# First difference of relu'd blocks kept in its PSUM bank, the transposes of the next batch moved into second products, weight stores at other times

## The chip, the cores and the metric

The kernel runs on one core of one Trainium2 chip. The metric is device time in microseconds (us) of one launch. The kernel before took 1024.24, 1024.7 and 1025.53 us in three runs; their median is 1024.7.

The engines have the names of the profile: PE multiplies matrices (PEld loads its weights), DVE and ACT work elementwise and can read and write PSUM, POOL works elementwise on SBUF, SP issues the transfers (DMA). PSUM has eight banks that matmuls of 128 x 384 results use here.

## The reference

Four batches of 768 tokens, eight heads of 64. Attention is restricted to keys of the query's own cluster; its result, heads side by side, is the input x (768 x 512 for each batch) of a second layer:

```
q_assign, k_assign = nearest of 16 centroids, by cosine
scores = where(q_assign == k_assign, q @ k.T / 8, -1e9)
x = softmax(scores) @ v                       # (4, 768, 512)
u = x + ((x.T @ U) @ V).T                     # mixes tokens, rank 32
out = u + maximum(u @ w1, 0) @ w2             # w1: 512 x 2048, w2: 2048 x 512
```

All is fp32. The kernel gets that precision out of the faster fp32r matmul by splitting an operand into a high and a low half, and adds three products (high x high, high x low, low x high).

## The kernel before, in words

The engines work in the order in which the program issues instructions to them; nothing reorders them. `at(time, fn, args)` puts a call into a plan, the plan is sorted by time, and the calls run in that order. The unit of the plan's time is one hidden chunk of the dense feed-forward (about 4.2 us, as 32 of them with their surroundings make up 466 to 635.7 us of the span); `M0` is that stage's start, `o` the start of a batch behind it. A plan's time decides order alone: an instruction starts when its engine reaches it and what it waits for is done.

There are three stages. **Attention**, 0 to 466 us, isn't touched. **Dense feed-forward of batch 0**, 466 to 635.7 us: in two halves of 384 tokens, 16 hidden chunks each, `gemm1` (L592), `after_gemm1` (L603: ReLU and split) and `gemm2` (L610) follow one another. Beside it the weights of the groups g = 2 and 3 are rebuilt from 64-bit words (`load_weights`, L178: joins on DVE at L162 to L172, high half on ACT at L190, low half on DVE at L191). Beside it, too, weights are prepared for the third stage. **Batches 1 to 3**, 635.7 to 1018 us, are computed by seven products on 2 x 2 blocks (Strassen in Winograd's form) instead of eight.

*Weights for the seven products.* For each of eight pairs n = 0 to 7 (group g, matrix k), `recover` (L656) adds high and low halves of four blocks (ACT copies one to PSUM at L659, DVE adds the other at L660), `combine` (L662) forms four sums on POOL, `split_high` (L673, ACT) and `split_low` (L678, POOL, L680) split them, `store_sum` (L682) stores them to DRAM from SP. Plain blocks are stored by `store_block` (L641). The sums lie in a buffer `f` in two places: even n and n = 7 share one, so that n = 7 waits for n = 6's stores. `fetch_w1` and `fetch_w2` bring the stored weights back, for one K at a time.

*Tokens for the seven products.* `fetch_half` brings 384 tokens of the next batch into the one buffer `st`; `turn_half` (L739) transposes them, three transposes a call into a bank (L742) and a copy by ACT (L743). `u_sums` (L749, DVE), and `u_halves` (L757: high half on ACT, low half on POOL, L761 and L766) form four sums and all halves of the seven left blocks. The first products need them in the order B11, T2, T3, T1, B21, T4, B22.

*A batch.* K counts eight blocks of hidden units. First products (1,K): seven groups of six matmuls (`seven1`, L799 to L801), one bank each. `after1` (L803) adds products with one another on DVE as they come; the results are the four relu'd blocks of hidden values, B11 and B22 through an ACT ReLU into SBUF, B12 and B21 left raw in their banks. `h_sums` (L834) then forms T1 = relu(B12) - B11, T3 = relu(B12) - B22, T2 = B22 - T1, T4 = relu(B21) - T2 on DVE (L838), and `h_halves` (L840) splits the seven blocks (ACT the high half, L845 and L848; the low half DVE for B21, L846, POOL for the others, L849). Second products (2,K): seven groups of six matmuls (`seven2`, L863 to L865), whose results `after2` (L872) adds to the output on DVE (L883) or copies at the first K of some accumulators on ACT (L881). The order in a batch is (1,0) (1,1) (1,2) (2,0) (1,3) (2,1) (1,4) (2,2) (1,5) (2,3) (1,6) (2,4) (1,7) (2,5) (2,6) (2,7). After the batch eight joins (`join_up`, L910, on DVE and POOL) make its output blocks; they stand in the first part of the next batch.

*Banks.* `bank()` (L730) hands the eight PSUM banks out in rotation, to product groups and, in batches 1 and 2, to the transposes of the next batch. A group waits until the bank's former tenant has been read for the last time: so the eighth call after raw B22's needs B22's bank, and each `turn_half` among them makes that an earlier group. `ring()` (L726) does the same for SBUF buffers of 128 x 384, and `spare` hands out pairs of buffers for high and low halves.

Of the kernel before, what the change touches and what calls it, by code (L numbers as in the profile page):

```python
# [34 lines left out]
AF = mybir.ActivationFunctionType  # L35
# [82 lines left out]
def clustered_attention_moe(ctx: ExitStack, tc: tile.TileContext, qk, v, cen, moe_U, moe_V, w1, w2, out):  # L118
# [3 lines left out]
    nc = tc.nc  # L122
# [570 lines left out]
    def pieces(x, n):  # L693
        return [x[:, k * n:(k + 1) * n] for k in range(x.shape[1] // n)]
# [21 lines left out]
    def open_right():  # L716

        pool["w3"].close()
        right = ctx.enter_context(tc.tile_pool(name="right", bufs=1, side="right", reuse_waits="tile"))
        acc = [rows.tile([P, 2, 2, HS], F32, name="acc", tag="R"), right.tile([P, 2, 2, HS], F32, name="acc2")]  # L720
        pool["acc"] = {key: acc[k // 2][:, k % 2] for k, key in enumerate((B11, T1, T3, T2))}
        pool["ring"] += pieces(right.tile([P, 4 * HS], F32, name="ring"), HS)
        spare.extend(pool["h"])
        spare.extend(right.tile([P, 2, HS], F32R, name=f"h{k}") for k in range(7))

    def ring():  # L726
        count["f"] += 1
        return pool["ring"][count["f"] % len(pool["ring"])]
# [74 lines left out]
    def after1(b, K, s):  # L803

        key = order[0][s]
        ps = live.pop(("p", b, K, key))
        h = live.setdefault(("f", b, K), {})
        add = nc.vector.tensor_add
        if key == B11:
            h["s"] = ring()  # L810
            nc.scalar.copy(h["s"], ps)
        elif key == T2:
            h["a"] = ring()
            add(h["a"], ps, h["s"])
        elif key == T3:
            h["b"] = ring()
            add(h["b"], ps, h["a"])
        elif key == T1:
            add(h["a"], ps, h["a"])
            add(ps, ps, h["b"])  # L820
            h["2"], h[B22] = ps, ring()
            nc.scalar.activation(h[B22], ps, AF.Relu)
        elif key == B21:
            add(ps, ps, h["s"])
            h[B11] = h["s"]
            nc.scalar.activation(h[B11], ps, AF.Relu)
        elif key == T4:
            add(ps, ps, h["b"])
            h[B21] = ps
        else:  # L830
            add(ps, ps, h["a"])
            h[B12] = ps

    def h_sums(b, K, key):  # L834
        h = live["f", b, K]
        one, two = {T1: (B12, B11), T3: (B12, B22), T2: ("2", T1), T4: (B21, T2)}[key]
        h[key] = ring()
        nc.vector.scalar_tensor_tensor(out=h[key], in0=h[one], scalar=0.0, in1=h[two], op0=ALU.max, op1=ALU.subtract)  # L838

    def h_halves(b, K, key):  # L840
        x = live["f", b, K][key]
        out_ = live["h", b, K, key] = spare.pop(0)
        hi, lo = out_[:, 0], out_[:, 1]
        if key == B21:
            nc.scalar.activation(hi, x, AF.Relu)  # L845
            nc.vector.scalar_tensor_tensor(out=lo, in0=x, scalar=0.0, in1=hi, op0=ALU.max, op1=ALU.subtract)  # L846
        else:
            nc.scalar.copy(hi, x)  # L848
            nc.gpsimd.tensor_sub(lo, x, hi)  # L849

    def unit2(b, e):
# [167 lines left out]
        at(m + (16.35 if i == 0 else 16.47), finish, i)  # L1019

    for n_, (g, k) in enumerate((g, k) for g in range(NG) for k in range(2)):
        c = M0 + 1.5 + 3.2 * n_
        for r in range(4):
            at(c + 0.4 * r, recover, n_, k, g, r)
            at(c + (0.9, 1.4, 1.75, 2.1)[r], combine, n_, r)
            at(c + (1.9, 2.25, 2.6, 2.8)[r], split_high, n_, r)
            at(c + (2.4, 2.7, 3.0, 3.3)[r], split_low, n_, r)
            at(c + (2.8, 3.1, 3.4, 3.7)[r], store_sum, n_, k, g, r)
        for r, name in enumerate(("A11", "A12", "A22")):
            for half in range(2):  # L1030
                x = 2 * r + half
                since = (95, 142, M0 - 9, M0 - 2.5)
                at(since[n_] + (6 if g == 0 else 0.9) * x if g < 2 else M0 + 1 + 4.1 * (n_ - 2) + 0.65 * x,
                   store_block, k, g, name, half)

    at(M0 + 18, open_sevens)
# [3 lines left out]
    for b in range(1, B):  # L1040
        o = M0 + NF * nh + 28 * (b - 1)
        if b == 1:
            fetched, turns = (o - 13.9, o - 6.4), (o - 7.7, o - 5.4)
        else:
            fetched, turns = (o - 20, o - 14), (o - 17.2, o - 9.7)
        for h in range(2):
            at(fetched[h], fetch_half, b, h)
            for d in range(ND):
# [9 lines left out]
        for k, (which, x) in enumerate(seq):  # L1058
# [7 lines left out]
                    at(t + U * s, seven2, b, m, e)  # L1066
                    at(t + U * s + 0.27, after2, b, m, e)
            if which == 1:
                for key, when_ in ((B22, 1.2), (B11, 1.45), (B21, 1.7)):
                    at(t + when_, h_halves, b, x, key)  # L1070
                for r, key in enumerate((T1, T3, T2, T4)):
                    at(t + 1.81 + 0.14 * r, h_sums, b, x, key)
                    at(t + (2.0, 2.15, 2.3, 2.56)[r], h_halves, b, x, key)
                if x + 2 < 8 or b < B - 1:
                    for s0, s1 in ((0, 4), (4, 7)):
                        at(t + U * s1 + 0.02, fetch_w1, (x + 2) % 8, s0, s1)
# [7 lines left out]
                at(o + 28 + when_, join_up, b, j)  # L1084
    for K in range(2):
        for s0, s1 in ((0, 4), (4, 7)):
            at(M0 + 23 + K, fetch_w1, K, s0, s1)
            at(M0 + (29.5 + 0.5 * K if s0 == 0 else 31.8 + 0.1 * K), fetch_w2, K, *range(s0, s1))

    plan.sort(key=lambda event: event[:2])  # L1090
    for _, _, fn, args in plan:
# [31 lines left out]
```

## Time and profile before

| | |
|---|---|
| median of three runs | 1024.7 us |
| profiled execution, its own time | 1025.75 us |
| its span | 1024.0 us |
| granted clock of PE, mean | 0.977 |
| busy PE / DVE / POOL / ACT | 962.9 / 709.2 / 624.1 / 471.5 us |
| DMA | 205.28 MB, 200 GB/s mean |

Rows of groups read: line of the kernel, engine, operation, what it writes <- what it reads, size, count, then busy time and the mean of one, then the engine's idle time just ahead of such instructions and what ended most of it. In a timeline a row begins with its start and its length, and ends in brackets with the idle time ahead of it and its releaser. Tiles have the program's names: ps_p and ps_q are the two name groups of the eight banks, st, f, u, h, hx, w, ring, rw, rw_g, rw_t SBUF buffers (several are buffers of earlier work used again), wc the stored weights in DRAM, u_scr the tokens in DRAM. Granted clock is the share of full speed that PE had in that stretch. Sums over stages hide much: PE's idle time is in few places, so it is read stretch by stretch.

### The profile page before, as it was taken

What the parts mean: (1) busy time and instruction counts of PE and PEld (TensorE: products, weight loads), DVE (VectorE), ACT (ScalarE), POOL (GpSimd) and SP (SyncE); (2) the same over time, 40 slices, a digit from 0 to 9 for tenths busy, and PEclk for the clock granted to TensorE, in tenths of its full rate; (3) what the DMA queues carried; (4) which work ended last, traced back from release to release, by engine and by line L of the source; (5) the groups of instructions that cost most, each with busy time, mean ns of one, the idle gap of its engine ahead of it and who ended that gap; (6) DMA issues with size and microseconds to landing.
All of it is one profiled execution on the core that took longest, in us unless ns stands there. A gap on an engine that the chain in (4) does not pass through costs nothing. (4 is left out here: it accounts for less than half of the span.)

```text
span 1024.0 us, 15360 instructions
## 1 busy us (share of the span) xinstructions
PE 962.9 (94%) x5368; PEld 785.0 (77%) x5368; DVE 709.2 (69%) x1298; ACT 471.5 (46%) x837; POOL 624.1 (61%) x477
## 2 busy tenths in 40 slices
PE   5899999999999999988898999999899998999997
PEld 3666676666667666656676879999899998999997
DVE  5797777777777767677867424746497665876767
ACT  4454554555556554564555434543244432344330
POOL 5466676988788967753545757634286533767431
PEclk9899999999999999989999999999999999999999
DMA  7754654656475646254688995775568775777743
GB/s 183 193 129 109 161 145 106 198 157 160 123 223 150 151 114 196 73 192 127 216 294 271 298 329 216 246 278 206 216 220 294 273 272 178 254 261 259 261 145 143
DMA packets 76732, 205.28 MB, mean 200 GB/s; under 512 B 8624, under 2 KB 42416, under 8 KB 71792
## 3 DMA queue, kind: packets, MB, share of 16 engines
q1 hardware_dynamic: 73968, 195.82, 59.9%
q10 hardware_dynamic: 2688, 8.49, 2.8%
q8 instruction: 42, 0.69, 0.3%
q14 instruction: 34, 0.28, 0.1%
HBM read 131.07 MB, written 41.94 MB: 169 GB/s over the span
## 5 line engine op out<-in xcount | busy, mean ns | idle before, releaser
L479 POOL TENSOR_TENSOR T<-T,pr 128x768 f32<-128x768 f32 x120 | 226.5, 1887 | 46.7 <-ACT pr L469 20.5
L442 DVE TENSOR_REDUCE m<-ps_max 128x1 f32<-128x384 f32 x384 | 195.3, 548 | 84.0 <-PE ps_max L440 82.4
L469 ACT ACTIVATE pr<-st 128x768 f32<-128x768 f32 x192 | 154.4, 812 | 86.2 <-PE st L466 69.5
L440 PE MATMUL ps_max<-arena 128*128 128x384 f32 x384 | 127.2, 381 | 6.7 <-DVE oh L356 2.5
L487 PE MATMUL o_ps<-pr,vt 128*64 128x384 f32 x768 | 133.1, 497 | 0.1
L464 PE MATMUL st<-arena 128*128 128x384 f32 x384 | 105.9, 357 | 1.8 <-ACT pr L469 1.8
L440 PEld LDWEIGHTS ps_max<-arena 128*128 128x128 f32 x384 | 70.9, 193 | 45.2 <-issue 22.0
L487 PEld LDWEIGHTS o_ps<-pr,vt 128*64 128x64 f32 x768 | 53.0, 139 | 67.1 <-issue 61.3
L466 PE MATMUL st<-arena 97*128 97x384 f32 x384 | 100.2, 343 | 3.7 <-DMA arena<-mT 1.9
L479 POOL TENSOR_TENSOR T<-pr 128x768 f32<-128x768 f32 x30 | 56.5, 1885 | 64.2 <-ACT pr L469 64.2
L464 PEld LDWEIGHTS st<-arena 128*128 128x128 f32 x384 | 66.8, 192 | 17.7 <-issue 9.9
L466 PEld LDWEIGHTS st<-arena 97*128 97x128 f32 x384 | 70.8, 191 | 5.7 <-issue 3.9
L491 ACT COPY os<-o_ps 128x384 f32<-128x384 f32 x32 | 15.3, 479 | 105.6 <-PE o_ps L487 105.6
L799 PE MATMUL ps_p<-arena,w 128*128 128x384 f32 x178 | 59.8, 336 | 0.0
L801 PE MATMUL ps_p<-arena,w 128*128 128x384 f32 x178 | 59.6, 335 | 0.0
L800 PE MATMUL ps_p<-arena,w 128*128 128x384 f32 x178 | 59.6, 335 | 0.0
L799 PE MATMUL ps_q<-arena,w 128*128 128x384 f32 x158 | 53.6, 339 | 0.0
L801 PE MATMUL ps_q<-arena,w 128*128 128x384 f32 x158 | 52.9, 335 | 0.0
L800 PE MATMUL ps_q<-arena,w 128*128 128x384 f32 x158 | 52.9, 335 | 0.0
L849 POOL TENSOR_TENSOR h<-ring,h 128x384 fp32r<-128x384 f32 x21 | 21.5, 1031 | 36.0 <-ACT h L848 19.5
L380 POOL TENSOR_TENSOR arena<-R,arena 128x768 fp32r<-128x768 f32 x18 | 34.5, 1923 | 13.6 <-ACT arena L375 8.0
L607 DVE SCALAR_TENSOR_TENSOR hx<-ps_h,hx 128x384 fp32r<-128x384 f32 x32 | 17.7, 553 | 27.4 <-ACT hx L606 27.2
(479 smaller groups left out, 2462.3 us busy)
## 6 DMA issues: line engine op xcount, KB each, us to landing
w<-wc SPq DMA_DIRECT2D x24, 1024.0 KB
w<-wc SPq DMA_DIRECT2D x24, 768.0 KB
wc<-f SPq DMA_DIRECT2D x52, 256.0 KB
arena<-wc SPq DMA_DIRECT2D x17, 768.0 KB
R<-in_qk SPq DMA_DIRECT2D x32, 384.0 KB
arena<-arena SPq DMA_DIRECT2D x32, 384.0 KB
arena<-arena SPq DMA_DIRECT2D x64, 192.0 KB
arena<-wc SPq DMA_DIRECT2D x10, 1024.0 KB
```

Source lines behind the costliest of these rows:

```text
L380: eng.tensor_sub(part(X2[i % 3], 0, h), live["R", i][:, 2 * h:2 * h + 2].rearrange("p j q -> p (j q)"), part(X1[i % 3], 0, h))
L440: nc.tensor.matmul(ps[:, 0:HS], x1[:, 0, g // 2, g % 2, t * P:(t + 1) * P], x1[:, 1, h, g % 2, :], start=True, stop=True)
L442: nc.vector.reduce_max(live["m2", i][:, h, u:u + 1], ps[:, 0:HS], axis=AX.X)
L464: nc.tensor.matmul(st[:, j, 0:HS], x1[:, 1, hk, j, ks], x1[:, 0, h, j, :], start=True, stop=False)
L466: nc.tensor.matmul(st[:, j, 0:HS], x2[0:97, 1, hk, j, ks], x2[0:97, 0, h, j, :], start=False, stop=True)
L469: nc.scalar.activation(pr, st[:, :, 0:HS], AF.Exp, scale=SCALE)
L479: eng.tensor_add(T, live["p", i, h, 0] if c == 1 else T, live["p", i, h, c])
L487: nc.tensor.matmul(o_ps[64 * j:64 * j + 64, 0:HS], vv[:, c, j, :], pr[:, j, :], start=(c == 0), stop=(c == NT - 1))
L799: nc.tensor.matmul(ps, w[:, 0, k], u[:, 0, k], start=(k == 0), stop=False)
L800: nc.tensor.matmul(ps, w[:, 0, k], u[:, 1, k], start=False, stop=False)
L801: nc.tensor.matmul(ps, w[:, 1, k], u[:, 0, k], start=False, stop=(k == 1))
L849: nc.gpsimd.tensor_sub(lo, x, hi)
```

## The change

1. `after1` frees raw B22's bank after its ReLU; `h_sums` writes T1 over raw B12, in B12's own bank, after T3 has read B12; T2 is a plain difference of relu'd B22 (SBUF) and T1 (PSUM). One ring buffer fewer is taken for each K, and the ring's counter is set when the ring grows.
2. `h_halves` is divided into `h_high` (ACT) and `h_low`. The low half of B21 moves from plan time 1.7 to 2.6, behind the four sums; T1's low half moves from POOL to DVE, and reads PSUM there.
3. The transposes of the next batch (batches 2 and 3) move from o - 17.2 and o - 9.7 to o - 15.7 and o - 8.7: from the first products (1,4) and (1,6) of the batch before into its second products (2,2) and (2,4).
4. Weight sums n = 0 to 6 move from M0 + 1.5 + 3.2n to M0 + 3 + 3.1n (n = 0 by +1.5, n = 6 by +0.9), n = 7 from M0 + 23.9 to M0 + 26.3. The plain blocks of n = 4 to 7 are stored from M0 + 15.5, 18.8, 22.1, 25.4 instead of M0 + 9.2, 13.3, 17.4, 21.5. The first fetches of w1 and w2 for K = 1 and of w2 for K = 0 move 1 to 2 units later.

```diff
@@ open_right
+        count["f"] = 13
@@ after1
             add(ps, ps, h["b"])
-            h["2"], h[B22] = ps, ring()
+            h[B22] = ring()
             nc.scalar.activation(h[B22], ps, AF.Relu)
@@
     def h_sums(b, K, key):
         h = live["f", b, K]
-        one, two = {T1: (B12, B11), T3: (B12, B22), T2: ("2", T1), T4: (B21, T2)}[key]
-        h[key] = ring()
-        nc.vector.scalar_tensor_tensor(out=h[key], in0=h[one], scalar=0.0, in1=h[two], op0=ALU.max, op1=ALU.subtract)
+        stt = nc.vector.scalar_tensor_tensor
+        if key == T1:
+            h[T1] = h[B12]
+            stt(out=h[T1], in0=h[B12], scalar=0.0, in1=h[B11], op0=ALU.max, op1=ALU.subtract)
+        elif key == T2:
+            h[T2] = ring()
+            nc.vector.tensor_sub(h[T2], h[B22], h[T1])
+        else:
+            h[key] = ring()
+            one, two = {T3: (B12, B22), T4: (B21, T2)}[key]
+            stt(out=h[key], in0=h[one], scalar=0.0, in1=h[two], op0=ALU.max, op1=ALU.subtract)

-    def h_halves(b, K, key):
+    def h_high(b, K, key):
...
+    def h_low(b, K, key):
...
+        elif key == T1:
+            nc.vector.tensor_sub(lo, x, hi)
         else:
-            nc.scalar.copy(hi, x)
             nc.gpsimd.tensor_sub(lo, x, hi)
@@ the plan
-        c = M0 + 1.5 + 3.2 * n_
+        c = M0 + (3 + 3.1 * n_ if n_ < 7 else 26.3)
...
-                at(since[n_] + (6 if g == 0 else 0.9) * x if g < 2 else M0 + 1 + 4.1 * (n_ - 2) + 0.65 * x,
+                at(since[n_] + (6 if g == 0 else 0.9) * x if g < 2 else M0 + 15.5 + 3.3 * (n_ - 4) + 0.55 * x,
                    store_block, k, g, name, half)
...
-            fetched, turns = (o - 20, o - 14), (o - 17.2, o - 9.7)
+            fetched, turns = (o - 20, o - 14), (o - 15.7, o - 8.7)
...
-                for key, when_ in ((B22, 1.2), (B11, 1.45), (B21, 1.7)):
-                    at(t + when_, h_halves, b, x, key)
-                for r, key in enumerate((T1, T3, T2, T4)):
-                    at(t + 1.81 + 0.14 * r, h_sums, b, x, key)
-                    at(t + (2.0, 2.15, 2.3, 2.56)[r], h_halves, b, x, key)
+                for key, sums, high, low in ((B22, None, 1.2, 1.25), (B11, None, 1.45, 1.5), (B21, None, 1.7, 2.6),
+                                             (T3, 1.81, 2.0, 2.1), (T1, 1.95, 2.15, 2.4), (T2, 2.09, 2.3, 2.35),
+                                             (T4, 2.23, 2.56, 2.6)):
+                    if sums:
+                        at(t + sums, h_sums, b, x, key)
+                    at(t + high, h_high, b, x, key)
+                    at(t + low, h_low, b, x, key)
...
-            at(M0 + 23 + K, fetch_w1, K, s0, s1)
-            at(M0 + (29.5 + 0.5 * K if s0 == 0 else 31.8 + 0.1 * K), fetch_w2, K, *range(s0, s1))
+            at(M0 + 23 + 3 * K, fetch_w1, K, s0, s1)
+            at(M0 + (30.5 + 0.5 * K if s0 == 0 else 31.8 + 0.1 * K), fetch_w2, K, *range(s0, s1))
```

What it does to DVE's order at the end of (1,4) of batch 1 and in (2,2), first before. The names end in a number for each buffer or bank; ps_p_6921 is raw B21, ps_q_6932 raw B12, ps_q_6895 raw B22 here:

```order
L828 TENSOR_TENSOR ps_p_6921<-ps_p_6921,rw_t_5002 128x384
L846 SCALAR_TENSOR_TENSOR u1_5004<-ps_p_6921,u1_5004 128x384
L831 TENSOR_TENSOR ps_q_6932<-ps_q_6932,rw_t_5001 128x384
L838 SCALAR_TENSOR_TENSOR ring_6435<-ps_q_6932,rw_g_5893 128x384
L838 SCALAR_TENSOR_TENSOR ring_6435<-ps_q_6932,ring_6435 128x384
L883 TENSOR_TENSOR f_5008<-ps_q_6947,f_5008 128x384
L838 SCALAR_TENSOR_TENSOR ring_6435<-ps_q_6895,ring_6435 128x384
L838 SCALAR_TENSOR_TENSOR rw_5890<-ps_p_6921,ring_6435 128x384
L883 TENSOR_TENSOR f_5008<-ps_p_6960,f_5008 128x384
```

And now, where ps_q_6905 is raw B21, ps_p_6916 first raw B12 and then T1, and h3_6439 and u1_5004 hold low halves:

```order
L829 TENSOR_TENSOR ps_q_6905<-ps_q_6905,rw_t_5002 128x384
L832 TENSOR_TENSOR ps_p_6916<-ps_p_6916,rw_t_5001 128x384
L847 SCALAR_TENSOR_TENSOR ring_6435<-ps_p_6916,ring_6435 128x384
L840 SCALAR_TENSOR_TENSOR ps_p_6916<-ps_p_6916,rw_g_5867 128x384
L896 TENSOR_TENSOR f_5008<-ps_q_6926,f_5008 128x384
L843 TENSOR_TENSOR ring_6435<-ring_6435,ps_p_6916 128x384
L847 SCALAR_TENSOR_TENSOR ring_6435<-ps_q_6905,ring_6435 128x384
L896 TENSOR_TENSOR f_5008<-ps_q_6943,f_5008 128x384
L860 TENSOR_TENSOR h3_6439<-ps_p_6916,h3_6439 128x384
L896 TENSOR_TENSOR acc_6433<-ps_q_6960,acc_6433 128x384
L858 SCALAR_TENSOR_TENSOR u1_5004<-ps_q_6905,u1_5004 128x384
```

B21's low half (L846, now L858) went from second place to the end, T3 stands ahead of T1, T1's low half (L860) is new on DVE, and nothing behind B12's sum reads raw B22.

The same at (2,0) of batch 2, where joins of batch 1 (L923) stand between; the order now, with ps_q_7803 raw B21 and ps_p_7815 raw B12, then T1:

```order
L829 TENSOR_TENSOR ps_q_7803<-ps_q_7803,ring_6435 128x384
L923 TENSOR_TENSOR f_5008<-f_5008,acc_6433 128x2x384
L832 TENSOR_TENSOR ps_p_7815<-ps_p_7815,ring_6435 128x384
L923 TENSOR_TENSOR acc2_6434<-acc2_6434 128x768
L847 SCALAR_TENSOR_TENSOR ring_6435<-ps_p_7815,ring_6435 128x384
L840 SCALAR_TENSOR_TENSOR ps_p_7815<-ps_p_7815,rw_g_5867 128x384
L896 TENSOR_TENSOR f_5008<-ps_q_7826,f_5008 128x384
L843 TENSOR_TENSOR rw_5864<-ring_6435,ps_p_7815 128x384
L923 TENSOR_TENSOR f_5008<-f_5008,acc2_6434 128x2x384
L847 SCALAR_TENSOR_TENSOR rw_5864<-ps_q_7803,rw_5864 128x384
L896 TENSOR_TENSOR f_5008<-ps_p_7842,f_5008 128x384
L923 TENSOR_TENSOR f_5008<-f_5008,acc2_6434 128x2x384
```

Behind these rows follow T1's low half (L860) and B21's low half (L858); the joins stand between the same sums as before, but B21's low half was ahead of the second of them.

On POOL, at the start of batch 1, before (arena_102 are the low halves of batch 1's tokens):

```order
L671 TENSOR_TENSOR f_5008<-f_5008 128x512
L680 TENSOR_TENSOR f_5008<-f_5008 128x512
L680 TENSOR_TENSOR f_5008<-f_5008,rw_t_5001 128x512
L680 TENSOR_TENSOR f_5008<-f_5008,rw_t_5002 128x512
L680 TENSOR_TENSOR f_5008<-f_5008 128x512
L761 TENSOR_TENSOR arena_102<-f_5008,arena_102 128x768
L766 TENSOR_TENSOR arena_102<-rw_5890,arena_102 128x384
L766 TENSOR_TENSOR arena_102<-rw_5891,arena_102 128x384
L761 TENSOR_TENSOR arena_102<-f_5008,arena_102 128x768
```

And now:

```order
L762 TENSOR_TENSOR arena_102<-f_5008,arena_102 128x768
L669 TENSOR_TENSOR f_5008<-f_5008 128x512
L671 TENSOR_TENSOR f_5008<-f_5008 128x512
L767 TENSOR_TENSOR arena_102<-rw_5864,arena_102 128x384
L767 TENSOR_TENSOR arena_102<-rw_5865,arena_102 128x384
L680 TENSOR_TENSOR f_5008<-f_5008 128x512
L680 TENSOR_TENSOR f_5008<-f_5008,rw_t_5001 128x512
L762 TENSOR_TENSOR arena_102<-f_5008,arena_102 128x768
L680 TENSOR_TENSOR f_5008<-f_5008,rw_t_5002 128x512
L767 TENSOR_TENSOR arena_102<-rw_5865,arena_102 128x384
L767 TENSOR_TENSOR arena_102<-rw_g_5866,arena_102 128x384
L680 TENSOR_TENSOR f_5008<-f_5008 128x512
```

Six of n = 7's operations (L669, L671 and four L680) stand among the low halves of batch 1's tokens; before, all stood ahead of the first of them.

More of the change, by code (lines that the diff above doesn't have):

```diff
@@ L835, in h_sums @@
         h = live["f", b, K]
-        one, two = {T1: (B12, B11), T3: (B12, B22), T2: ("2", T1), T4: (B21, T2)}[key]
-        h[key] = ring()
-        nc.vector.scalar_tensor_tensor(out=h[key], in0=h[one], scalar=0.0, in1=h[two], op0=ALU.max, op1=ALU.subtract)
-    def h_halves(b, K, key):
-        x = live["f", b, K][key]
-        out_ = live["h", b, K, key] = spare.pop(0)
-        hi, lo = out_[:, 0], out_[:, 1]
+        stt = nc.vector.scalar_tensor_tensor
[10 more added lines that the diff above has]
+    def h_high(b, K, key):
+        x = live["f", b, K][key]
+        hi = (live.setdefault(("h", b, K, key), spare.pop(0)))[:, 0]
+        nc.scalar.activation(hi, x, AF.Relu if key == B21 else AF.Copy)
+    def h_low(b, K, key):
+        x = live["f", b, K][key]
+        hi, lo = (live["h", b, K, key][:, k] for k in range(2))
         if key == B21:
-            nc.scalar.activation(hi, x, AF.Relu)
             nc.vector.scalar_tensor_tensor(out=lo, in0=x, scalar=0.0, in1=hi, op0=ALU.max, op1=ALU.subtract)
+        elif key == T1:
+            nc.vector.tensor_sub(lo, x, hi)
         else:
-            nc.scalar.copy(hi, x)
             nc.gpsimd.tensor_sub(lo, x, hi)
```

## The prediction

> **What bounds the kernel now.** I read the page first, then busy time by stage, then every idle stretch of PE, then the rows around those stretches on DVE, ACT and POOL. Share of the span, then the three stretches that the change touches (columns: us, then busy us of PE, PEld, DVE, ACT, POOL, then granted clock, DMA share, GB/s):
>
> ```profile
> PE 962.9 (94%) x5368; PEld 785.0 (77%) x5368; DVE 709.2 (69%) x1298; ACT 471.5 (46%) x837; POOL 624.1 (61%) x477
> 466.00:564.00 98.00, 84.14 (x400) 67.97 (x399) 73.20 (x120) 50.72 (x99) 47.48 (x37) 0.97 0.70 229
> 564.00:635.70 71.70, 69.27 (x348) 61.35 (x347) 27.66 (x39) 30.03 (x60) 50.68 (x40) 0.98 0.86 301
> 635.70:1007.00 371.30, 356.72 (x2015) 352.69 (x2014) 251.99 (x450) 140.13 (x302) 190.69 (x173) 0.98 0.66 235
> ```
>
> PE bounds the kernel; the change leaves its matmuls as they are, so it can win only PE's idle time and half-clock time. From 635.7 on 14.6 us are idle (371.30 - 356.72). The timeline of PE puts most of it in front of one kind of matmul, the first one into a PSUM bank that an earlier reader still holds (start, length, and in brackets the idle time and its releaser):
>
> ```profile
> 664.63 0.45 PE L863 MATMUL ps_q<-w,arena 128*128 128x384 f32 x1 [0.68 <-DVE rw_t L838]
> 695.41 0.44 PE L863 MATMUL ps_q<-h,arena 128*128 128x384 f32 x1 [1.98 <-DVE ring L838]
> 729.46 0.44 PE L863 MATMUL ps_q<-u,arena 128*128 128x384 f32 x1 [3.03 <-DVE rw L838]
> 795.56 0.69 PE L863 MATMUL ps_q<-h,arena 128*128 128x384 f32 x1 [2.04 <-DVE rw_t L838]
> 827.90 0.45 PE L863 MATMUL ps_q<-h,arena 128*128 128x384 f32 x1 [2.00 <-DVE ring L838]
> 860.39 0.69 PE L863 MATMUL ps_q<-h,arena 128*128 128x384 f32 x1 [3.03 <-DVE rw L838]
> 926.30 0.44 PE L863 MATMUL ps_q<-u,arena 128*128 128x384 f32 x1 [1.20 <-DVE rw_t L838]
> ```
>
> These are (2,0), (2,2), (2,4) of batch 1, the same three of batch 2, and (2,0) of batch 3. The releaser is always L838, the sums T1 to T4, which read the banks of raw B22 and B21. Idle time has a second price. PE alone around 695 and around 828 (PE busy, granted clock, DMA share, GB/s):
>
> ```profile
> 693.08:696.49 3.41, 1.43 (x9) 1.00 0.43 178
> 696.49:699.90 3.41, 3.41 (x13) 0.50 0.00 0
> 699.90:703.31 3.41, 3.41 (x21) 1.00 0.38 83
> 826.19:829.61 3.42, 1.71 (x10) 1.00 0.23 95
> 546.31:549.72 3.41, 3.37 (x8) 0.50 0.79 279
> 604.33:607.74 3.41, 3.41 (x9) 0.50 1.06 378
> ```
>
> After the stretch with 1.98 idle, the next 3.41 us run at 0.50: 13 matmuls instead of 21, 8 x 0.176 = 1.4 us lost. So a gap of 2 to 3 us costs up to 4.4 us. The equal gap at 827.90 is divided between two such stretches and I find no 0.50 behind it; I find one behind 729.46, 795.56 and 860.39, none behind 0.68 or 1.20. The Trainium skill ("TensorE: Matmul & The Clock Gate", "Why this matters for your kernels") advises to avoid PE-idle gaps over about 3 us; by that, gaps of 2 us would cost no clock and the sum below would lose about 4 us. The trace disagrees: 0.50 after 1.98.
>
> **The four stalls with transposes, (2,2) and (2,4) of batches 1 and 2.** Around the first, from the end of (1,4):
>
> ```profile
> 690.84 0.49 PE L742 MATMUL ps_p<-ident,st 128*128 128x128 f32 x3
> 691.37 0.48 ACT L743 COPY f<-ps_p 128x384 f32<-128x384 f32 x1 [0.45 <-PE ps_p L742]
> 691.75 0.50 ACT L845 ACTIVATE u<-ps_p 128x384 fp32r<-128x384 f32 x1
> 692.28 0.56 DVE L846 SCALAR_TENSOR_TENSOR u<-ps_p,u 128x384 fp32r<-128x384 f32 x1 [1.71 <-ACT u L845]
> 692.75 0.56 DVE L831 TENSOR_TENSOR ps_q<-ps_q,rw_t 128x384 f32<-128x384 f32 x1
> 693.41 0.56 DVE L838 SCALAR_TENSOR_TENSOR ring<-ps_q,rw_g 128x384 f32<-128x384 f32 x1
> 693.88 0.55 DVE L838 SCALAR_TENSOR_TENSOR ring<-ps_q,ring 128x384 f32<-128x384 f32 x1
> 694.35 0.55 DVE L883 TENSOR_TENSOR f<-ps_q,f 128x384 f32<-128x384 f32 x1
> 694.81 0.55 DVE L838 SCALAR_TENSOR_TENSOR ring<-ps_q,ring 128x384 f32<-128x384 f32 x1
> 692.22 0.34 PE L863 MATMUL ps_p<-h,arena 128*128 128x384 f32 x1
> 693.10 0.34 PE L865 MATMUL ps_p<-hx,arena 128*128 128x384 f32 x1
> ```
>
> PE starts a matmul each 0.176 us ((693.10 - 692.22) / 5), so a group of six is 1.05, and three transposes take 0.25 (691.09 would be the next start). The third group wanted to start at 693.27 and needs the bank of raw B22, read last by T2 (694.81). DVE was idle 1.71 because B21's low half L846 waits for ACT L845, which stood behind the transposition's copy L743; B12's sum L831, of a group that ended at 690.84, queued behind it. DVE's step is 0.47 between independent sums and 0.66 where an operation reads the sum just ahead of it.
>
> After: T1 lies in B12's bank, B22's bank is free after its ReLU, B21's low half goes to the end of the chain, and the transposes stand inside (2,2) and (2,4): e0 t0 e1 t1 e2 e3 t2 e4 e5 t3 e6 (e a group of the second products, t three transposes). The rotation now makes t2 want the bank of raw B21. DVE's chain, from the end of the first products' last group: B12's sum 0, T3 0.66, T1 1.13, e0's sum 1.60, T2 2.07, T4 2.73, e1's 3.20, T1's low half 3.67, e2's 4.14, B21's low half 4.61 to 5.17. PE gets to t2 after four groups and two transposes, 4.20 + 0.50 = 4.70, less one matmul, since PE starts the next while the last one still runs: 4.53. It waits about 0.7, too short for the clock by the rows of 664.63 and 926.30. Gone: 1.98 + 3.03 + 2.00 + 3.03 = 10.04 idle and three half-clock stretches, 4.2; new: 4 x 0.7 = 2.8. **Net -11.4.** Bounds for t2's wait: 0 and 2.0 (three operations of 0.47 later). No group but t2 has this wait: without transposes B21's bank is wanted by the seventh group at 6.1, with the chain done at 5.2.
>
> **(2,0).** Batch 1: 0.68 goes, as there the bank is wanted at 6.1: **-0.7**. Batches 2 and 3 have joins of the previous batch in DVE's chain:
>
> ```profile
> 790.04 0.95 DVE L910 TENSOR_TENSOR f<-f,acc 128x768 f32<-128x768 f32 x1
> 795.43 2.62 DVE L910 TENSOR_TENSOR f<-f,acc 128x768 f32<-128x768 f32 x1
> 792.79 4.44 POOL L910 TENSOR_TENSOR f<-f,acc 128x768 f32<-128x768 f32 x2
> ```
>
> A join of the same shape takes 0.95, or 2.62 while POOL runs one too. The Trainium skill ("SBUF — State Buffer", "SBUF: two separate sides") states that DVE's operations with two SBUF sources and GpSimd's SBUF accesses lock each other out; the two rows agree. It would not touch T1's low half, which reads PSUM. Four joins stand in front of B21's low half. Without a clash it ends at 5.17 + 0.35 (what the first delays B12's sum) + 3 x 0.95 - 0.47 (e2's sum is no DVE work in (2,0)) - 2 x 0.19 (joins fill the 0.66 steps) = 7.5, 1.4 after PE wants the bank (6.1), and up to 6.4 after it with three joins at 2.62 (3 x 1.67 = 5.0 more). I take two clashes, 3.2 idle and most of a half-clock stretch, 1.1: 4.3 in place of 2.04 + 1.4. **+0.9** (range -2.0 to +4.4). In batch 3 two fewer sums of e stand ahead (0.94): 0.5 to 5.5; I take 2.3 + 0.8 in place of 1.20, **+1.9** (-0.7 to +5.7).
>
> **The weight stores and the start of batch 1 (564 to 636).** The last sums of weights, n=7:
>
> ```profile
> 602.07 0.69 DVE L660 TENSOR_TENSOR f<-ps_r,w2h 128x512 f32<-128x512 f32 x1 [7.97 <-DMA wc<-f]
> 603.84 0.33 PE L742 MATMUL ps_uT<-ident,st 128*128 128x128 f32 x1 [1.90 <-ACT f L743]
> 613.42 0.30 PE L742 MATMUL ps_uT<-ident,st 128*128 128x128 f32 x1 [0.52 <-DMA st<-u_scr]
> 612.56 1.27 POOL L680 TENSOR_TENSOR f<-f 128x512 fp32r<-128x512 f32 x1
> 631.76 1.33 POOL L766 TENSOR_TENSOR arena<-rw_g,arena 128x384 fp32r<-128x384 f32 x1
> 633.04 2.31 POOL L766 TENSOR_TENSOR arena<-rw_t,arena 128x384 fp32r<-128x384 f32 x2
> 635.68 0.34 PE L799 MATMUL ps_p<-arena,w 128*128 128x384 f32 x1
> ```
>
> DVE waits 7.97 for a store out of buffers that n=6 and n=7 share; through ACT's queue PE waits 1.90 and loses the stretch at 604.33. With n=7 at 26.3 instead of 23.9 the stores are out in time: -1.9 - 1.4 = -3.3. But six POOL operations of n=7 (L669, L671, four L680) now stand after B11's low half among the low halves of batch 1's sums: 6 x 1.27 = 7.6. T3's second half ends at 634.2 (half of the 2.31), and the third group wants it at 635.68 + 2.10 = 637.8: slack 3.6, lateness up to 4.0. Some of it falls into POOL's idle time ahead of these halves, so I take 3.0 and most of a stretch, 1.1: +4.1. **Net +0.8** (-3.3 to +4.0). The 0.52 for `st` stays. The blocks of n=4 to 7 go to SP later, past the fetches of w1 and st; DMA share is 0.86 here, so they cost nothing while the queue has 0.14 to spare, and about the 0.5 of the st row per fetch if not. The fetch for (2,0) moves one unit of about 4.2 us later and is wanted over 20 us after it.
>
> **The earlier stretch (466 to 564), 13.9 idle.** Starting n=0 at 3 instead of 1.5 with 3.1 between takes sums L660 from in front of the joins of weights that PE waits for:
>
> ```profile
> 545.45 0.50 PE L617 MATMUL y<-w2h,hx 128*128 128x512 f32 x1 [2.22 <-ACT w2h L190]
> 542.03 0.69 DVE L660 TENSOR_TENSOR f<-ps_r,arena 128x512 f32<-128x512 f32 x1 [0.71 <-ACT ps_r L659]
> ```
>
> At this place one L660 stands ahead instead of three: two steps of 0.69 and the 0.71 of waiting, 2.1 earlier, and the stretch at 546.31 with it: -3.5. Elsewhere a sum moved later can land in front of a join. **-3** (-6 to +1).
>
> T1's low half puts 24 operations of 0.47 on DVE, busy 252 of 371, and takes as many from POOL; both lie beside PE except where the chains above count them. One buffer fewer per product costs nothing while PE is the bound; its cover is the same margin.
>
> **Sum:** -11.4 - 0.7 + 0.9 + 1.9 + 0.8 - 3.0 = -11.5. The profiled execution (1025.75) stands 1.05 above the median, 1024.7; from the median this gives 1013.
>
> **Rivals.** A: the joins all clash and n=7 costs batch 1 all of 4.0 + 1.4. For it: 2.62 is in the trace, and the six operations stand where order puts them. Against: POOL's joins overlap only some of DVE's now. +3.5 + 3.8 + 1.3 = 8.6 more: 1021. B: the earlier stretch gives nothing (its joins wait for DMA instead), and t2 waits 1.0: 1017. C, slower: B21's low half, now last behind T1's, keeps its bank too long at all 18 places where second products follow first ones (six in each of three batches). The margin is 6.1 - 5.2 = 0.9; at a chain x later it costs (x - 0.9) x 18 and eats the 11.5 from x = 1.5, about three operations of 0.47 more. At 1.9, 18.0 - 11.5: about 1030. Against: the chain has idle slots between e0, e1, e2. D: half-clock stretches do not follow from these gaps, -4.2 and the like are void: 1017. E: t2 never waits and the earlier stretch gives all 6: 1006. F: the change does not free the bank; but in the order of before the raw bank of B22 has two sums, ReLU and T2, and now T2 reads ReLU's result, so I give it no chance.
>
> **Chances.** The sum's case 0.60, A 0.15, B 0.08, D 0.04, E 0.06, C 0.07. About 0.2% (2.05 us) is what a measurement tells from no change: faster below 1022.65, slower above 1026.75. C is slower, 0.07; a third of A's 0.15, the part in which its prices come out higher still, lies within the 0.2%, 0.05; the rest is faster, 0.88. The range goes from just under E's 1006 to A's 1021; outside stay C, that part of A, and some 0.06 of the sum's own tails.
>
> **What would show it.** Right: no L863 with over 1 us in front in (2,2) and (2,4) and no 0.50 behind them; a short wait before a transpose late in each; (2,0) of batches 2 and 3 waiting for L858; no 7.97 in front of L660; a wait of about 3 us at batch 1's third group, released by POOL. Wrong: stalls in every (2,x) (C), or batch 1's start over 5 us late (A).

## The result and the profile after

The changed kernel took 1010.42 us (median of 1008.38 to 1012.2), the kernel before 1024.47 on the same chip: a ratio of 0.986, 95% interval 0.9835 to 0.9885. That is 14.05 us less; 1013 was forecast, in a range from just under 1006 to 1021. The profiled execution took 1008.9, 1.5 under the median, with a span of 1007.1 in place of 1024.0. So the traces differ by 16.9, and the attribution below, read from them, adds up to that: 2.8 more than the medians differ by, as the profiled execution before (1025.75) lies above the four timed runs of its kernel, and the one after near the lowest of its own. All medians here and below leave out four runs of 1330 to 3030 us, far above all others of the same kernel.

Busy time of each engine over the span, then in three stretches of the new profile (us, then busy us of PE, PEld, DVE, ACT, POOL, then clock, DMA share, GB/s):

```profile
PE 953.1 (95%) x5368; PEld 778.0 (77%) x5368; DVE 715.1 (71%) x1322; ACT 472.0 (47%) x837; POOL 601.5 (60%) x453
466.00:560.00 94.00, 82.16 (x398) 66.96 (x397) 71.51 (x119) 48.63 (x94) 43.69 (x34) 0.98 0.64 207
560.00:634.80 74.80, 69.48 (x342) 62.15 (x342) 29.25 (x40) 31.96 (x64) 50.61 (x39) 0.95 0.80 273
634.80:990.00 355.20, 349.64 (x2014) 346.56 (x2013) 256.94 (x475) 140.08 (x302) 172.61 (x153) 1.00 0.71 256
```

The products (last row) run at a clock of 1.00 with 5.6 us idle. In the stretch in front of them (second row) the clock fell to 0.95, and 5.3 us are idle. The timeline of PE has these waits behind 600 us (start, length, and in brackets the idle time and its releaser):

```profile
606.98 0.30 PE L743 MATMUL ps_uT<-ident,st 128*128 128x128 f32 x1 [3.09 <-DMA st<-u_scr]
631.09 0.70 PE L617 MATMUL y<-w2h,hx 128*128 128x512 f32 x1 [2.23 <-ACT hx L606]
693.86 0.33 PE L743 MATMUL ps_q<-ident,st 128*128 128x128 f32 x1 [0.40 <-DVE u L858]
725.03 0.33 PE L743 MATMUL ps_q<-ident,st 128*128 128x128 f32 x1 [0.40 <-DVE arena L858]
789.35 0.44 PE L876 MATMUL ps_q<-u,arena 128*128 128x384 f32 x1 [2.81 <-DVE h L858]
817.84 0.33 PE L743 MATMUL ps_q<-ident,st 128*128 128x128 f32 x1 [0.41 <-DVE w2l L858]
849.04 0.33 PE L743 MATMUL ps_q<-ident,st 128*128 128x128 f32 x1 [0.38 <-DVE h L858]
911.59 0.44 PE L876 MATMUL ps_q<-u,arena 128*128 128x384 f32 x1 [1.02 <-DVE hx L858]
```

The four stalls of 2 to 3 us became waits of 0.4, in front of a transpose, released by B21's low half L858: the place, the bank and the releaser that the forecast named. The stalls of (2,0) in batches 2 and 3 stayed, with L858 as releaser. The waits at 607 and 631 are new; the 1.90 at 603.84 of before is gone.

Where the time went, as the start of each place on PE in the profile after less the same in the profile before:

| place | after - before, us | step |
|---|---|---|
| first gemm1 of batch 0 | -0.6 | -0.6 |
| its chunk 16 of 32 | -3.5 | -2.9 |
| chunk 20 | -5.0 | -1.5 |
| (1,0) of batch 1 | -0.8 | +4.2 |
| (2,0) of batch 1 | -0.4 | +0.4 |
| (1,4) of batch 1 | -1.4 | -1.0 |
| (1,7) of batch 1, behind (2,2) and (2,4) | -8.9 | -7.5 |
| (1,4) of batch 2 | -9.9 | -1.0 |
| (1,7) of batch 2, behind (2,2) and (2,4) | -15.8 | -5.9 |
| (1,0) of batch 3 | -16.6 | -0.9 |
| end of the span | -16.9 | -0.2 |

The stalls with transposes gave 13.4. The stretch up to chunk 20 gave 5.0, of which 0.6 stands ahead of all that was changed, and 4.2 was lost again before batch 1 began.

### The profile page after: what moved, and what is told of

Its sections match the earlier page's. It is cut to its first block, busy times and chain, and to the rows that moved or that the text cites. A ratio compares the mean times of both kernels' runs of the same rounds, so it can differ in the third digit from the quotient of the medians.

```text
span 1007.1 us, 15377 instructions
## 1 busy us (share of the span) xinstructions
PE 953.1 (95%) x5368; PEld 778.0 (77%) x5368; DVE 715.1 (71%) x1322; ACT 472.0 (47%) x837; POOL 601.5 (60%) x453
## 5 line engine op out<-in xcount | busy, mean ns | idle before, releaser
L800 PE MATMUL ps_p<-arena,w 128*128 128x384 f32 x186 | 62.3, 335 | 0.1
L801 PE MATMUL ps_p<-arena,w 128*128 128x384 f32 x186 | 62.2, 334 | 0.0
L802 PE MATMUL ps_p<-arena,w 128*128 128x384 f32 x186 | 62.2, 334 | 0.0
L800 PE MATMUL ps_q<-arena,w 128*128 128x384 f32 x150 | 50.1, 334 | 0.0
L802 PE MATMUL ps_q<-arena,w 128*128 128x384 f32 x150 | 50.1, 334 | 0.0
L801 PE MATMUL ps_q<-arena,w 128*128 128x384 f32 x150 | 50.1, 334 | 0.0
L665 POOL TENSOR_TENSOR f<-f 128x512 f32<-128x512 f32 x8 | 10.3, 1293 | 52.1 <-DVE f L660 52.1
## 6 DMA issues: line engine op xcount, KB each, us to landing
w<-wc SPq DMA_DIRECT2D x24, 1024.0 KB
arena<-wc SPq DMA_DIRECT2D x10, 1024.0 KB
```

Of the source, the lines that this page charges most:

```text
L800: nc.tensor.matmul(ps, w[:, 0, k], u[:, 0, k], start=(k == 0), stop=False)
L801: nc.tensor.matmul(ps, w[:, 0, k], u[:, 1, k], start=False, stop=False)
L802: nc.tensor.matmul(ps, w[:, 1, k], u[:, 0, k], start=False, stop=(k == 1))
```

## Experiments

Times are medians, ratios go by the runs of the kernel before on the same chip. The chips differ, so kernels that ran on different chips are best compared by their ratios.

**The products' part alone.** The changed kernel with the four plan lines on weights put back:

```diff
-        c = M0 + (3 + 3.1 * n_ if n_ < 7 else 26.3)
+        c = M0 + 1.5 + 3.2 * n_
(and store_block, fetch_w1, fetch_w2 as before)
```

> The changed kernel with the plan times of weight sums, weight stores and first fetches of before: what the products' part (T1 in its bank, the order of DVE's chain, the transposes' place) gives alone. By the two traces the products' part gave 16.0 of the 16.85 between the profiled executions (start of batch 1 stands 0.84 earlier, the end 16.85): if the parts add, 1008.5. By the forecast's terms for it (-11.4 - 0.7 + 0.9 + 1.9 = -9.3): 1015.2. In the profile: 1.90 in front of a transpose near 604 and the half-clock stretch behind it as before, no wait over 0.5 in (2,2) and (2,4).

Measured: 1010.0 against 1022.75, ratio 0.9871 (0.9853 to 0.9889); its profiled span is 15.7 under that of before. Within the intervals the products' part is the whole gain. The waits in (2,2) and (2,4) are 0.37 to 0.41. One thing came otherwise than expected: the wait near 603 is 1.61, and no half-clock stretch follows it in this execution, so batch 1 starts 1.1 earlier than before, which isn't the products' doing.

**The weight times alone.** The opposite: the kernel before with these lines alone.

> The kernel before with the changed plan times of weight sums, stores and first fetches alone. If the parts add, as the traces have it: batch 1 starts about 0.8 earlier and nothing else moves, 1023.6. By the forecast (-3.0 + 0.8): 1022.3. In the profile: a sum of batch 1's tokens on DVE waits some 3 for the store out of rw_t, and PE some 2 behind ReLU of the last hidden chunk; the seven stalls of the products stay.

Measured: 1024.38 against 1022.75, ratio 1.0023 (1.0006 to 1.0039): nothing gained, by the interval a little lost. The profile tells why. Batch 1 starts 3.3 earlier than before, and then its (1,2) waits for w1 of K = 2, which shifts its (2,0) to 3.4 later:

```profile
652.83 0.69 PE L799 MATMUL ps_p<-arena,w 128*128 128x384 f32 x1 [2.93 <-DMA w<-wc]
```

So it loses 2.93 and what the half-clock time behind it costs (6.8 us at 0.50, from 652.2). In the changed kernel PE reaches the same matmul at 651.83, and 0.15 ahead of it are idle: the transfer lands just in time. What fills the queues is the fetch of w2 for K = 0: in the changed order it stands behind n = 7's stores on SP and starts at 634.06 in the changed kernel and 634.65 here, instead of 618.92. Before, DMA was idle from 636 to 640; now it is full up to 652. The rows below are of PE alone (us, PE busy, clock, DMA share, GB/s), first of the kernel before, then of the changed kernel, then of this one:

```profile
636.00:640.00 4.00, 4.00 (x22) 1.00 0.00 0
```

```profile
636.00:640.00 4.00, 4.00 (x22) 1.00 0.95 379
648.00:652.00 4.00, 3.85 (x23) 1.00 1.00 416
```

```profile
648.00:652.00 4.00, 1.90 (x11) 1.00 1.02 413
```

**The move of the transposes alone**, on the kernel before:

```diff
-            fetched, turns = (o - 20, o - 14), (o - 17.2, o - 9.7)
+            fetched, turns = (o - 20, o - 14), (o - 15.7, o - 8.7)
```

> The kernel before with the transposes of the next batch moved into (2,2) and (2,4), nothing else. Theory P (the place of the transposes made the stalls: they moved the bank rotation on by one group and put ACT's copy in front of B21's high half): raw B22's bank is wanted by the third group, 2.6 after the first products end, and T2's sum is done 2.6 after B12's sum starts, so gaps of at most 0.5 are left, no half-clock stretch behind them: 1024.5 - 8.5 - 4.2 = 1012. Theory F (raw B22's bank, held until T2, made them): the bank is still held, gaps of 2 and more stay, 1021 to 1025.

Measured: 1011.69 against 1022.75, ratio 0.9895 (0.9877 to 0.9913). Theory P holds, with 0.8 left where it allowed 0.5. The stalls are still at the same kind of matmul with L838 as releaser, so the bank is still held, but they are short, and no half-clock stretch follows any of them:

```profile
691.28 0.44 PE L863 MATMUL ps_q<-h,arena 128*128 128x384 f32 x1 [0.81 <-DVE ring L838]
722.94 0.45 PE L863 MATMUL ps_q<-h,arena 128*128 128x384 f32 x1 [0.84 <-DVE rw L838]
...
817.27 0.45 PE L863 MATMUL ps_q<-h,arena 128*128 128x384 f32 x1 [0.84 <-DVE ring L838]
848.94 0.45 PE L863 MATMUL ps_q<-u,arena 128*128 128x384 f32 x1 [0.79 <-DVE rw L838]
```

**The bank alone**: the products' part with the transposes where they were.

```diff
-            fetched, turns = (o - 20, o - 14), (o - 15.7, o - 8.7)
+            fetched, turns = (o - 20, o - 14), (o - 17.2, o - 9.7)
```

> The products' part without the move of the transposes: T1 in B12's bank, B22's bank free after its ReLU, B21's low half last, transposes in (1,4) and (1,6) as before; weight stores as before. Theory F: no group waits for raw B22 any more and DVE's chain starts without ACT, so the four stalls go all the same; raw B21's bank is then wanted by the sixth group at 5.3, its low half done at 5.2: about 1024.5 - 14 = 1010.5. Theory P: with the transposes still there ACT's copies stay in front and gaps of 1 to 2 are left with two or three half-clock stretches, 1017.

Measured: 1008.82, ratio 0.9866 (0.9844 to 0.9887). Theory F holds as well: two waits of 0.4 are left (724.75 and 849.76, both released by L858). Either half of the products' change removes the long stalls; together they give no more than the bank's half alone. From the start of (1,4) to that of (1,7), batches 1 and 2 together, the profiles gained 13.4 with both, 11.4 with the transposes alone, 14.4 with the bank alone. Which one the change needed was open after the forecast; the answer is neither in particular. The two theories were rivals on paper only: a stall needed a bank wanted early and a reader that finishes late, and each half cures one of them. The bank's half itself holds two things, T1 in B12's bank and B21's low half at the end of the chain; no run has them apart, so which of the two it needs isn't shown.

**A buffer of n = 7 under batch 1's sums.** On the changed kernel DVE waits in front of the second half of T3, one of the sums of batch 1's tokens, and the ReLU that PE needs (L606) stands behind that sum's copy in ACT's queue:

```profile
628.34 1.70 DVE L756 TENSOR_TENSOR rw_t<-f 128x384 f32<-128x384 f32 x1 [2.91 <-DMA wc<-rw_t]
630.13 0.51 ACT L766 CAST arena<-rw_t 128x384 fp32r<-128x384 f32 x1 [4.15 <-DVE rw_t L756]
630.55 0.48 ACT L606 ACTIVATE hx<-ps_h 128x384 fp32r<-128x384 f32 x1
```

The ring of SBUF buffers contains the two rw_t out of which n = 7's sums are stored. The edit turns the ring by one place:

```diff
-    spare, count = [], {"bank": 0, "f": 0, "o": 0}
+    spare, count = [], {"bank": 0, "f": 7, "o": 0}
```

> The changed kernel with the ring of SBUF buffers turned on by one place before batch 1 (its counter starts at 7 instead of 0), so that the fourth sum of batch 1's tokens (T3's second half) is written to rw_g and no longer to rw_t, out of which a late store of n=7 still reads; the two sums of T4 get rw_t. Theory R (the 2.91 that DVE waits there, by way of ACT's queue, makes PE's 2.23 at 631 and the half-clock stretch behind it): both go, batch 1 starts some 3 earlier, about 1007.5. Rival Q (ACT and DVE are late there because POOL and SP are, whichever buffer): the wait moves on to T4's first sum and PE's wait stays within 1 of 2.23, 1010.

Measured: 1012.98, ratio 0.9909 (0.9886 to 0.9933), by its ratio 0.5% above the changed kernel, with intervals that just don't meet; why it would be slower isn't shown. The mechanism is as theory R has it: 2.23 and its half-clock stretch are gone, batch 1 starts at 630.54, 4.3 earlier. The time isn't: (1,2) comes to the same transfer as in the kernel with the weight times alone.

```profile
608.26 0.30 PE L743 MATMUL ps_uT<-ident,st 128*128 128x128 f32 x1 [3.48 <-DMA st<-u_scr]
636.34 0.45 PE L801 MATMUL ps_p<-arena,w 128*128 128x384 f32 x1 [1.14 <-POOL arena L767]
651.98 0.44 PE L800 MATMUL ps_p<-arena,w 128*128 128x384 f32 x1 [2.59 <-DMA w<-wc]
```

(1,3) starts at 666.68, in the changed kernel at 666.52. Whatever is won ahead of 652 is lost there, because w1 of K = 2 lands at 652. (The first row, a wait for st, is taken up at the end.)

**The joins later.** Four of the eight joins behind B21's low half:

```diff
-            for j, when_ in enumerate((0.02, 0.1, 5, 5.3, 5.1, 5.45, 5.6, 5.9)):
+            for j, when_ in enumerate((0.02, 0.1, 5, 6.55, 5.1, 6.6, 6.75, 7.05)):
```

> The changed kernel with four of the eight joins behind a batch (acc2's sum, the one into y12, those into y21 and y22) 1.15 to 1.25 units later, behind B21's low half in DVE's order at (2,0). Theory J (the joins between the four sums, slowed by POOL's, keep B21's bank): 2.81 in front of (2,0)'s last group in batch 2 and 1.02 in batch 3 fall under 0.5, nothing new: 1010.4 - 3.0 = 1007.4, more where a half-clock stretch followed. Rival: the joins land on DVE's adds of (1,3) and the wait is taken there, or the output stores now behind the fetch of weights make a transfer late: 1010.

Here and in the kernel of all three edits below, batch 2's joins come after batch 3 has begun to fill the same accumulators, so batch 2's output differs, and what is won at (2,0) of batch 3 isn't to be had; the work of every engine is the same. Measured: 1006.31, ratio 0.9844 (0.9816 to 0.9873), 4.1 under the changed kernel's median, but by the ratios only 0.0016 of some 1020, 1.6 us, with intervals that overlap. The traces decide: no wait is left at (2,0) of batches 2 and 3. DVE's chain in the changed kernel and, below it, POOL's joins beside it:

```profile
781.05 1.30 DVE L923 TENSOR_TENSOR acc<-acc 128x768 f32<-128x768 f32 x1
784.14 1.72 DVE L923 TENSOR_TENSOR f<-f,acc 128x768 f32<-128x768 f32 x1
786.72 1.65 DVE L923 TENSOR_TENSOR f<-f,acc 128x768 f32<-128x768 f32 x1
788.75 0.54 DVE L858 SCALAR_TENSOR_TENSOR h<-ps_q,h 128x384 fp32r<-128x384 f32 x1
781.50 2.57 POOL L923 TENSOR_TENSOR f<-f,acc 128x768 f32<-128x768 f32 x1
785.00 2.54 POOL L923 TENSOR_TENSOR f<-f,acc 128x768 f32<-128x768 f32 x1
```

And L858 with the joins behind it:

```profile
785.73 0.55 DVE L858 SCALAR_TENSOR_TENSOR h<-ps_q,h 128x384 fp32r<-128x384 f32 x1
```

It ends 5.2 after (2,0) began (786.28 - 781.11), ahead of the 6.1 at which its bank is wanted; in the changed kernel it ended 9.2 after (789.29 - 780.09). The wait at 652 of the two kernels above is here too (2.54 at 651.44).

**The transfers in another order.** w1 of K = 1 later, w2 for K = 0 and 1 ahead of n = 7's stores:

```diff
-            at(M0 + 23 + 3 * K, fetch_w1, K, s0, s1)
-            at(M0 + (30.5 + 0.5 * K if s0 == 0 else 31.8 + 0.1 * K), fetch_w2, K, *range(s0, s1))
+            at(M0 + 23 + 4.6 * K, fetch_w1, K, s0, s1)
+            at(M0 + (28.6 + 0.45 * K if s0 == 0 else 31.8 + 0.1 * K), fetch_w2, K, *range(s0, s1))
```

> The changed kernel with transfers in another order on SP: the fetch of w1 for K=1 1.6 units later (behind the plain blocks of n=7), the first parts of w2's fetches for K=0 and 1 before n=7's stores of sums (28.6 and 29.05 instead of 30.5 and 31.0). Theory D (the transfers' own congestion: st's 6.7 us from issue to landing at 600, and the fetch of w1 for K=2 landing as it is needed at 652): the 3.09 at 607 falls to under 1.5, DMA is idle for some of 640 to 652 again and the 0.15 at 651.8 goes; against it stands the store out of rw_t, now behind more on SP, so that 2.23 at 631 may grow: about 1008, and runs closer together. Rival: st waits for its buffer or lane, not for bandwidth: 3.09 stays, 1010 or more.

Measured: 1010.39, ratio 0.9888 (0.9859 to 0.9917). Half of theory D: DMA's share in 648 to 652 falls to 0.59 and nothing waits there, but the wait for st stays at 2.98 (the rival's half), and 2.23 stays. Two half-clock stretches follow the 2.98. The runs lie no closer together (1009.66 to 1015.08).

**All three edits.**

> The three edits of the other kernels of this call together (ring, joins, transfers) on the changed kernel. If each does what its theory says, 3.09, 2.23 and 2.81 go with the half-clock stretches at 607 and 631: 1010.4 - 8.1 - 2.5 = 1000. If only the joins count: 1007.4.

Measured: 1004.75, ratio 0.9823 (0.9796 to 0.985), 5.7 under the changed kernel (3.8 by the ratios) where 10.4 was expected if each did its part. The waits at 631, 652 and at (2,0) are gone; the wait for st is 3.79 with two half-clock stretches, and a wait of 1.11 for POOL's low half of T1 to T4 appears at batch 1's start.

**The joins of batch 1 on the products' part alone.** The join edit for b = 1 only:

> The products' part of the change (weight sums, stores and fetches at the plan times of before) and the four joins later, for the joins of batch 1 only; batch 2's stay where they were, since batch 3's second products take the accumulators in another order and need them sooner. Theory J: 2.81 at (2,0) of batch 2 and the half-clock stretch behind it (0.8 to 1.5) go, 1.02 in batch 3 stays; with the 1010.0 of the products' part alone, 1006.2, every run under 1008.5. Rival: without the changed stores the gain of the early stretch is missed, and joins give what they gave on the changed kernel's median, 2.6: 1007.5.

Measured: 1005.43 against 1022.63, ratio 0.9831 (0.9809 to 0.9853), every run of the comparison under 1007.3. That is 4.6 under the products' part alone, whose ratio was 0.9871 (4.1 by the ratios). Theory J holds: the 2.81 and its half-clock stretch at (2,0) of batch 2 are gone, 1.02 in batch 3 stays.

**An earlier fetch into st.** Ring, joins of batch 1, transfers, and:

```diff
-            fetched, turns = (o - 13.9, o - 6.4), (o - 7.7, o - 5.4)
+            fetched, turns = (o - 13.9, o - 7.0), (o - 8.3, o - 5.4)
```

> The changed kernel with ring, transfers and batch 1's joins as tried, and the transposes of batch 1's first half 0.6 units earlier, so that st's second fetch can be issued some 2.5 earlier. Theory D2 (the fetch takes 6 to 7 us from issue to landing because the stores fill the queues, and only an earlier issue helps): the wait for st falls from 3 to 4 to about 1, the half-clock stretch behind it goes, start of batch 1 about 4 earlier than with the other edits alone: 1001. Rival (the first half's transposes now wait, as the buffer they are copied to is still being stored from n=5, or SP waits for PE with n=6's stores behind it): PE waits 2 to 3 near 595 instead, 1005.

Measured: 1002.7, ratio 0.9807 (0.9784 to 0.983), the fastest of all by its median. Its interval overlaps that of the kernel ahead, but on this chip each of its five runs (1004.63 at most) lies under each of that kernel's four (1004.83 at least). Theory D2 holds: from issue to the transposes that wait for it the transfer takes 7.2 here and 6.7 in the changed kernel, 4.9 before (DMA share meanwhile 1.07, 1.06 and 0.69), so it isn't faster, but issued at 596.37 instead of 600.24 it costs 0.42 instead of 3.09; no half-clock stretch follows, and batch 1 starts at 625.87, 9.8 ahead of before. What is left there is POOL:

```profile
603.60 0.30 PE L743 MATMUL ps_uT<-ident,st 128*128 128x128 f32 x1 [0.42 <-DMA st<-u_scr]
631.68 0.45 PE L801 MATMUL ps_p<-arena,w 128*128 128x384 f32 x1 [1.10 <-POOL arena L767]
```

**The same earlier transposes on the weight times of before.**

> The products' part with batch 1's joins, as the other kernel of this call, and the earlier transposes of batch 1's first half, on the weight times of before. There ACT copies for n=7's sums wait for n=6's stores at 594 to 602 and the transposes' copies stand behind them (1.61 at 603). If an earlier place in ACT's order lets the transposes by: 1.6 less, 1004.6. If the stall moves to the copies (they stand behind the same wait) or to st: 1006.2 and no change.

Measured: 1006.22, ratio 0.9835 (0.9812 to 0.9858), no better than 1005.43 without it. The wait at 603 went, but PE waits for ReLUs and their low halves behind it (0.57, 0.91, 0.74) and a half-clock stretch follows at 612. So in these runs the earlier fetch pays with the changed weight times and not without them, and the changed weight times pay only with all of it: with ring, joins and transfers but without the earlier fetch they gave a ratio of 0.9823, no clear gain on the 0.9831 of the weight times of before with the joins alone.

## Why the prediction was right, and where it was not

- **The four stalls**, -11.4 forecast, -13.4 in the trace. Idle time fell from 10.04 to 1.59 and the three half-clock stretches went. Of the 2.0 between forecast and trace, 1.2 is the wait for t2, forecast at 0.7 and measured at 0.4 in four places. The other 0.8 is the price of a half-clock stretch: what is left of the 13.4 behind idle time, 4.9, makes 1.6 to 1.7 for each of the three, half of 3.41, where the forecast had 1.4. The forecast priced the bank and the transposes as one thing; the runs showed that each is enough.
- **(2,0) of batch 1**: -0.7 forecast, -1.0 seen.
- **(2,0) of batches 2 and 3**: +0.9 and +1.9 forecast, -0.7 and -0.2 seen. The wait with joins in the chain came as described (2.81, three joins at 1.30 to 1.72). That 3.2 was forecast is in part luck: by the forecast's own prices two clashes make 1.4 + 2 x 1.67 = 4.7. Two terms were mis-sized. In batch 2 the half-clock stretch didn't follow in this execution; in the four other kernels with 2.8 at this place (the products' part alone, the bank alone, the ring, the transfers) it did, and in the products' part alone the place cost +0.7 (from -9.8 at (2,0) to -9.1 at (2,1)), near the +0.9. In batch 3 the joins behind the first took 1.02 to 1.31, so the wait was 1.02, near the lower bound of 0.5.
- **564 to 636, +0.8 and the earlier stretch, -3.0.** Early, the trace has -4.4 between the first gemm1 and chunk 20. At the place that the forecast named it has -3.4, with -3.5 forecast: from chunk 13 to chunk 14 PE took 9.19 before and 5.79 after, one L660 stands ahead of the joins and the stretch at 546 is gone. From chunk 20 to (2,0) of batch 1 it has +4.6. The 1.90 in front of a transpose and its half-clock stretch went, as forecast. The step that failed is the one on POOL: six operations among the low halves were to make T3 late for the third group at 637.8. That group starts at 639.04, since the last chunk of gemm2 lies between the second and the third group, a cover of 2.1 that the working missed; T3's second half ended 3.3 later than before (637.5 instead of 634.2) and was still in time. The price came by another way: n = 7's late store held a ring buffer (2.23 and a half-clock stretch, shown by turning the ring), and st's fetch was later than its transposes (3.09 and one, shown by fetching earlier). POOL's lateness is real and shows as 1.1 once batch 1 starts earlier. Also wrong: one unit of about 4.2 for the fetch of w2, and nothing to pay for it. It moved by 15.1 (618.92 to 634.06), because SP reached it behind n = 7's stores, which wait for POOL, and it left w1 of K = 2 to land no sooner than it is needed.
- **Waits for DMA** at 891 and 1010 (0.62 and 0.48), which the forecast doesn't name, are absent from the new profile. The first shows in the 0.9 of the table's last row but one, the second nowhere.
- **Rivals.** C didn't occur: no (2,1), (2,3) or (2,5) waits. D is out, since in every kernel in which the stalls of (2,2) and (2,4) went, the half-clock stretches behind them went too, and idle time alone leaves 4.9 of the 13.4 unexplained. (Two of the three stretches stood behind waits of 3.03; so gaps of 2 us account for 1.4 of the 4.2 there, not for about 4.) A's pieces were each found, smaller. B and E are out: the early stretch gave 4.4, neither nothing nor 6, and t2 waits 0.4, neither 1.0 nor never. By its own terms E makes 1013.2 - 2.8 - 3 = 1007.4, not 1006. F is out: no matmul of (2,2) or (2,4) waits for the bank of raw B22 any more, with the bank's half alone either.

The forecast's 1013 is 2.6 above the median, and the sum of -11.5 is near -14.05 partly by luck, as errors of both signs met. The products' terms were too careful: -9.3 forecast, -15.3 in the trace. The weight terms were too kind: -2.2 forecast together, +0.2 in the trace from the first gemm1 to (2,0) of batch 1, and +1.6 by the medians of that part alone.

## What to carry to other kernels

A stall on a buffer has two ends, the taker that comes early and the reader that finishes late; before pricing two cures as a sum, try each alone, as either may be the whole gain. What is won ahead of a transfer that lands at a fixed time is given back there, so look past the stall for the next arrival and at how full DMA is in between. A shared ring of buffers ties a late store to unrelated work: ask of each late store which buffer it holds and who takes that buffer next.

## What the hardware showed that was not expected

A wait of nearly 3 us doesn't always lead to a stretch at half clock: it depends on how it falls on a grid of stretches of 3.41 us. In the kernel before, stretches at 0.50 begin at 546.31, 604.33 and 696.49, and the 58.02 and 92.16 between them are 17 and 27 times 3.413. The 2.81 at (2,0) of batch 2 is divided in the changed kernel (1.69 and 1.12 idle) and costs no clock; in the kernel with the products' part alone the same 2.81 lies almost wholly in one (2.60) and does. Windows of PE alone, the changed kernel, then the other:

```profile
784.82:788.23 3.41, 1.72 (x10) 1.00 0.00 0
788.23:791.65 3.42, 2.30 (x13) 1.00 0.97 380
```

```profile
785.03:788.44 3.41, 0.81 (x5) 1.00 0.22 85
788.44:791.85 3.41, 3.20 (x10) 0.50 1.03 375
```

In the kernel with the ring turned even the 3.48 in front of 608.26 costs no clock: continued back from its stretch at 0.50 near 791, the grid divides it into 1.9 and 1.6. Against that stands the stall at 695.41 of before, 1.98 in one stretch, with 0.50 behind it. So the same program's time can differ by one such stretch, up to 1.7 us (half of 3.41), from where it falls. That the spread of the changed kernel's runs (1008.4 to 1012.2) comes from it wasn't shown.

The Trainium skill ("SBUF — State Buffer", "SBUF: two separate sides") states that DVE's operations with two SBUF sources and POOL's operations that read SBUF lock each other out. The traces agree that one of the two is held up, and show that it can be either. In the kernel before, DVE's join of 790.04 took 0.95, and POOL's low half beside it 1.45, where the next one took 1.02:

```profile
790.41 1.45 POOL L849 TENSOR_TENSOR w<-rw_g,w 128x384 fp32r<-128x384 f32 x1 [0.87 <-PE ps_q L865]
791.82 1.02 POOL L849 TENSOR_TENSOR h<-ring,h 128x384 fp32r<-128x384 f32 x1
```

Beside POOL's work DVE's joins at (2,0) of batches 2 and 3 took 1.02 to 1.72 in the changed kernel, 0.95 where nothing held them up. So the 2.62 of one join of before was near the upper end (another took 2.66, at 767.77), and the forecast's bound of three joins at 2.62 was far off.
